# A linear-attention and long-convolution kernel on one core: other first loads, one kind of inverse tile, a new order of all steps

## The chip, the cores and the metric

The kernel runs on one core of one Trainium2 chip. A core has TensorE (PE, with its weight loads PEld), VectorE (DVE), ScalarE (ACT) and GpSimd (POOL), and SyncE (SP), which here only issues transfers. Each runs its own instructions in their order and waits on semaphores for the others. The metric is the device time of one execution in microseconds (us); lower is better.

## The reference

Eight batches, eight heads, 576 positions. First a linear attention with feature maps made of exponentials, then a gated convolution over positions, done in the frequency domain:

```python
def phi(x):                                   # x: (8, 8, 576, 64), w_phi: (64, 128)
    proj = np.einsum('bhsd,df->bhsf', x, w_phi)
    proj = proj - np.max(np.abs(proj), axis=-1, keepdims=True)
    return np.concatenate([np.exp(proj), np.exp(-proj)], axis=-1)
q_p, k_p = (phi(q), phi(k))
kv = np.einsum('bhsf,bhsd->bhfd', k_p, v)
z = np.sum(k_p, axis=2)
num = np.einsum('bhsf,bhfd->bhsd', q_p, kv)
den = np.einsum('bhsf,bhf->bhs', q_p, z)[..., None] + 1e-06
x = num / den                                 # then laid out as (8, 576, 512)
...
proj = x @ w_proj                             # (512, 1536): x1, x2, x3
X2 = np.fft.rfft(x2, n=S, axis=1)
H = np.fft.rfft(filter_fft, n=S, axis=0)[None, :, :]
x2_conv = np.fft.irfft(X2 * H, n=S, axis=1)
out = (x1 * x2_conv * x3) @ w_out             # float32
```

## The kernel before

One batch after the other passes through a chain of steps, and the chains of neighbouring batches are interleaved. Nothing plans at run time: a long text, PLAN, names every step in the order in which it is issued, with its batch and tile, the engine where there is a choice, and the PSUM bank behind an @. run() goes through the words and calls the method of that name. Each engine executes its share of the words in this order; a step waits only for the data and buffers that it needs.

The steps of a batch b (tiles v, m or c run over 0 to 3):

- load and loadh bring q, k and v with a cast to bf16, from GpSimd's queue; loadh brings half the heads. They fill kn, qn and vn, two buffers each. trh (L602) transposes half a batch into kT or qT on SP's queue; for batch 0, pt and pte do it on TensorE with an eviction.
- Pk and Qn (matmuls with w_phi), then maxk and maxq (VectorE, the absolute maxima, L707); a suffix t is the tail of the 576 positions. mhi, mlo, trm and trme turn the maxima of q into mT, which Pq subtracts inside its own matmuls. ex (ScalarE, L693) takes exponentials of both signs. em scales by the maxima of k, vs (L749) scales v by it, KV and KVe make the 128 x 65 sums.
- NE, rc and xn divide numerator by denominator. trx (L816) and trxt (L821) transpose the result x into xT and xTt by transfer; in batch 0 ptx does three of four on TensorE.
- f1 and f2 (L846, L852) fold x, F and Fe transform it to frequencies (XF), X2 multiplies by the middle third of w_proj, Y1 multiplies by the filter's spectrum, m3 (L911) sums. X1 and X3 (L919) are the outer thirds, tm multiplies them into x1s.
- The inverse transform of a tile m of 128 channels comes in two kinds. I is six matmuls into two banks for even and odd parts; Ie copies one to SBUF on ScalarE (L990), Ip and Im add and subtract the other on VectorE (L993), and ym multiplies by x1s on GpSimd or VectorE (L1038). J is ten matmuls that give the sum and the difference at once (L1028), with four more rows of the constants inv made by gen_neg and gen_ends, and yj multiplies both by x1s in one VectorE instruction (L1032). 21 tiles are of the first kind and 11 of the second.
- O multiplies by w_out (L1049), Oe evicts the product into one of four buffers o, and st (L1058) writes it out in two halves from SP's queue, each half under its own transfer.

The filter is prepared once: eight fl_load and one fl_loadt (L476, L482) read it on SP's queue, fa (L488) adds and subtracts its mirrored parts on GpSimd, rev (L499) reverses by a float32 matmul, fb, ft, Ff and Ffe transform it, and H and He give the spectrum. Constants for the transforms are made on GpSimd (gi_*), VectorE (cols_*, ang, frac) and ScalarE (sin). wz are matmuls on zeros with no use of their result.

Of the kernel before, what the change touches and what calls it, by code (L numbers as in the profile page):

```python
# [37 lines left out]
pt,k,0,0,1@3 sin,0 maxq,0,0@4 Pk,0,0@0 pte,ACT,k,0,0,1@3 pt,k,0,1,1@6 fa,POOL,1 pt,k,0,1,0@7
maxk,0,0@0 pte,ACT,k,0,1,1@6 Qn,0,2@4 pte,ACT,k,0,1,0@7 pte,DVE,q,0,1,1@2 maxq,0,2@4 Pk,0,1@6
Qn,0,3@2 ft,POOL fa,POOL,0 maxq,0,3@2 ex,k,m,0,0@0 wz,9@4 Qnt,0@4 ex,k,p,0,0@0 maxqt,0@4 Pk,0,2@2  # L40
maxk,0,2@2 ex,k,m,0,1@6 Pk,0,3@4 w_load,proj,1 rev@0 ex,k,p,0,1@6 maxk,0,3@4 mhi,0 ex,k,p,0,2@2
maxk,0,1@6 ex,k,m,0,2@2 one Pkt,0@6 mlo,DVE,0 ex,k,m,0,3@4 trm,0@2 wz,1@3 maxkt,0@6 trh,q,1,0
fb,0@0 trme,ACT,0@2 wz,12@3 em,m,0,0 ex,k,p,0,3@4 vs,POOL,m,0,0 Pq,0,1@2 trh,q,1,1 fb,1@0 em,p,0,0
exkt,m,0@6 Pq,0,2@4 exkt,p,0@6 ex,q,m,0,1@2 wz,25@0 trh,k,1,0 vs,POOL,p,0,0 ex,q,p,0,1@2 Qn,1,0@0
wz,14@6 trh,k,1,1 em,m,0,1 ex,q,p,0,2@4 maxq,1,0@0 Pq,0,3@2 w_load,proj,2 KV,0,0@6 ex,q,m,0,2@4
vs,DVE,m,0,1 em,p,0,1 ex,q,p,0,3@2 Ff,1@4 vs,POOL,p,0,1 KVe,DVE,0,0@6 Pk,1,1@0 ex,q,m,0,3@2
Ffe,DVE,1@4 Qn,1,3@6 ex,k,m,1,1@0 maxq,1,3@6 NE,0,1@4 Ff,0@2 w_load,proj,0 maxk,1,1@0 KV,0,1@6
Ffe,ACT,0@2 load,v,1 rc,0,1@4 ex,k,p,1,1@0 gen_ends,POOL Pq,0,0@2 xn,0,1@4 KVe,DVE,0,1@6 Qnt,1@4
trx,0,1 ex,q,m,0,0@2 Pk,1,0@0 maxqt,1@4 Ff,2@6 load,k,2 ex,q,p,0,0@2 maxk,1,0@0 NE,0,3@4 load,q,2
Ffe,ACT,2@6 NE,0,0@2 rc,0,3@4 ex,k,p,1,0@0 xn,0,3@4 NE,0,2@6 rc,0,0@2 Pqt,0@4 xn,0,0@2 ex,k,m,1,0@0  # L50
rc,0,2@6 ptx,0,3@2 f1,POOL,0,0,0 xn,0,2@6 exqt,p,0@4 ptx,0,0@3 Ff,3@0 exqt,m,0@4 ptxe,DVE,0,3@2
ptx,0,2@6 ptxe,DVE,0,0@3 f1,POOL,0,0,1 Ffe,ACT,3@0 Qn,1,2@4 ptxe,DVE,0,2@6 Pk,1,3@2 maxq,1,2@4
NEt,0@0 ex,k,m,1,3@2 f1,POOL,0,1,0 Pkt,1@6 exkt,m,1@6 rct,0@0 wz,27@4 maxk,1,3@2 f2,POOL,0,0,0
exkt,p,1@6 X1,0,0@5 Hl,ACT maxkt,1@6 H,0@4 f2,POOL,0,0,1 ex,k,p,1,3@2 xnt,0,0@0 H,2@6 xnt,0,1@0
He,DVE,0,0@4 f1,POOL,0,1,1 Qn,1,1@0 em,m,1,0 He,ACT,2,0@6 Pk,1,2@2 maxq,1,1@0 H,1@7 X1e,ACT,0,0@5
# [140 lines left out]
class Kernel:  # L196
# [273 lines left out]

    def fl_load(self, i, a):
        self.nc.sync.dma_start(  # L476
# [638 lines left out]
```

## Time and profile before

| what | us |
|---|---|
| median of 3 runs | 312.28 |
| lowest and highest run | 309.18, 315.27 |
| span of the profiled execution, first to last instruction | 311.6 |

The profiled execution's time is known by its span alone, which lies 0.7 below the median of the runs and within their spread. In the profile a busy engine is one with an instruction in flight; matmuls overlap, so the busy time of PE is larger than the time that each adds to a queue of them. A group's line gives busy time and the mean of one, then the idle time of its engine ahead of it and what ended most of it. Rows of a timeline give start, length, engine and line; brackets at the end give the idle time ahead and what ended it. PEclk is the share of TensorE's full clock that was granted.

### The profile page before, as it was taken

How to read it: one execution, taken by the hardware profiler on the slowest of the kernel's cores; microseconds unless marked ns; L12 is line 12 of the kernel's file. 1: busy time of each engine (PE TensorE's matmuls, PEld its weight loads, DVE VectorE, ACT ScalarE, POOL GpSimd, SP SyncE). 2: the span in 40 equal slices, each digit the busy share in tenths (PEclk: the TensorE clock that was granted, in tenths of full speed). 3: DMA queues.
4: the chain of work that ended last, by engine and by line, in shares of the span. 5: the costliest groups of instructions: out<-in, count | busy, mean ns of one | idle time of the engine just before them, and what ended most of it. 6: DMA issues, size and time to landing. Idle time of an engine off the chain costs nothing.

```text
span 311.6 us, 10240 instructions
## 1 busy us (share of the span) xinstructions
PE 281.0 (90%) x4331; PEld 205.3 (66%) x4360; DVE 268.6 (86%) x447; ACT 216.3 (69%) x345; POOL 203.8 (65%) x163
## 2 busy tenths in 40 slices
PE   1968977999999996999899799999999999999992
PEld 0534665778667874687577677587578767786761
DVE  6997999699988884978897888799999999998863
ACT  1898997797668764499679469883837898834230
POOL 8446877668673975667958667977259877674040
PEclk9978999899999998999999999999999999999998
DMA  7999999799799869696695999998350252060046
GB/s 162 235 203 159 136 202 193 105 190 133 91 164 204 94 110 170 116 160 107 114 198 82 131 160 153 172 175 160 84 117 4 56 93 69 19 110 21 1 115 192
DMA packets 72735, 40.20 MB, mean 129 GB/s; under 512 B 53040, under 2 KB 67504, under 8 KB 72688
## 3 DMA queue, kind: packets, MB, share of 16 engines
q1 hardware_dynamic: 57472, 22.62, 40.2%
q0 software_dynamic: 14816, 16.25, 34.5%
q10 hardware_dynamic: 400, 0.66, 0.8%
q8 instruction: 34, 0.56, 0.8%
q14 instruction: 13, 0.11, 0.1%
HBM read 33.75 MB, written 9.44 MB: 139 GB/s over the span
## 4 chain that ended last, share of the span: by engine, by line
PE 70%; DVE 12%; DMA 7%; ACT 5%; issue 3%; SPq 1%; POOL 0%; DVEq 0%; POOLq 0%
PE ps L919 16%; PE ps L897 10%; PE ps L1049 8%; PE ps L764 5%; PE ps L972 4%; PE ps L778 4%; DMA xT<-xn 4%; DMA out_dram<-o 3%; PE ps L1028 3%; PE ps L858 3%; PE ps L862 3%; PE ps L928 2%; DVE mq L707 2%; PE ps L665 2%; PE ps L638 2%
## 5 line engine op out<-in xcount | busy, mean ns | idle before, releaser
L919 PE MATMUL ps<-xT,wproj 128*128 128x256 bf16 x512 | 65.8, 275 | 4.3 <-DVE x1s L960 2.3
L919 PEld LDWEIGHTS <-wproj 128*128 128x128 bf16 x512 | 48.6, 98 | 14.5 <-issue 5.1
L707 DVE TENSOR_REDUCE mk<-ps 128x8 f32<-128x1024 f32 (+1 forms) x40 | 44.0, 1110 | 5.9 <-ACT HTo L295 2.2
L707 DVE TENSOR_REDUCE mq<-ps 128x8 f32<-128x1024 f32 (+1 forms) x40 | 44.0, 1110 | 5.5 <-PE ps L638 4.5
L749 POOL TENSOR_TENSOR vm<-vn,vm 128x1152 bf16<-128x1152 bf16 x14 | 30.4, 2178 | 18.2 <-ACT vm L743 18.2
L749 POOL TENSOR_TENSOR vp<-vn,vp 128x1152 bf16<-128x1152 bf16 x16 | 34.8, 2180 | 10.5 <-ACT vp L743 10.3
L911 POOL TENSOR_TENSOR T<-T,T 128x1024 bf16<-128x1024 bf16 x12 | 25.5, 2124 | 21.9 <-DVE T L907 21.8
L693 ACT ACTIVATE Ekp<-ps 128x1024 bf16<-128x1024 f32 x32 | 32.8, 1030 | 6.6 <-DVE mk L707 3.3
L1038 POOL TENSOR_TENSOR yT<-cv,x1s 128x576 bf16<-128x576 f32 x19 | 24.3, 1289 | 18.3 <-DVE x1s L964 12.8
L852 POOL TENSOR_TENSOR xf<-SD 128x512 bf16<-128x512 bf16 x27 | 31.2, 1170 | 6.7 <-DVE SD L846 5.3
L693 ACT ACTIVATE Ekm<-ps 128x1024 bf16<-128x1024 f32 x32 | 32.8, 1033 | 3.6 <-DVE mk L707 2.7
L693 ACT ACTIVATE Eqm<-ps 128x1024 bf16<-128x1024 f32 x32 | 32.9, 1034 | 3.1 <-PE ps L671 2.9
L1049 PE MATMUL ps<-wout,yT 128*128 128x512 bf16 x133 | 34.3, 385 | 0.7 <-issue 0.2
L693 ACT ACTIVATE Eqp<-ps 128x1024 bf16<-128x1024 f32 x32 | 32.5, 1031 | 3.4 <-PE ps L671 3.3
L846 POOL TENSOR_TENSOR SD<-xn 128x512 bf16<-128x512 bf16 x23 | 26.5, 1160 | 12.6 <-DVE xn L797 12.6
L897 PE MATMUL ps<-wproj,XF 128*128 128x512 bf16 x117 | 30.3, 380 | 0.7 <-issue 0.2
L295 ACT CAST x1s<-ps 128x512 bf16<-128x512 f32 (+1 forms) x30 | 16.0, 548 | 13.1 <-PE ps L928 8.4
L797 DVE TENSOR_TENSOR xn<-ps,r 128x512 bf16<-128x512 f32 x32 | 22.0, 689 | 1.1
L1049 PEld LDWEIGHTS <-yT 128*128 128x128 bf16 x144 | 13.4, 99 | 14.1 <-issue 0.6
L990 ACT COPY es<-ps 128x288 f32<-128x288 f32 x21 | 8.5, 404 | 20.3 <-PE ps L972 19.8
L960 DVE TENSOR_TENSOR x1s<-ps,x1s 128x512 bf16<-128x512 f32 x32 | 21.7, 683 | 0.6 <-ACT x1s L295 0.4
L778 PE MATMUL ps<-KVs,Eqp 128*128 128x65 bf16 x256 | 19.6, 192 | 2.2 <-DVE mq L707 0.6
...
## 6 DMA issues: line engine op xcount, KB each, us to landing
out_dram<-o SPq DMA_DIRECT2D x67, 128.0 KB, 2.9
vn<-in_v_dram POOLq DMA_DIRECT2D x8, 576.0 KB, 7.5
kn<-in_k_dram POOLq DMA_DIRECT2D x7, 576.0 KB, 9.7
qn<-in_q_dram POOLq DMA_DIRECT2D x7, 576.0 KB, 6.6
...
fl<-in_moe_filter_fft_dram SPq DMA_DIRECT2D x8, 128.0 KB, 5.8
out_dram<-o ACTq DMA_DIRECT2D x5, 128.0 KB, 2.8
...
```

The lines of the kernel that those rows point to most:

```text
L693: self.nc.scalar.activation(e, p, AF.Exp, bias=0.0, scale=1.0 if g == "p" else -1.0)
L707: self.nc.vector.tensor_reduce(out=out, in_=src, axis=AX.X, op=ALU.max, apply_absolute_value=True)
L749: self.eng(eng).tensor_tensor(out=t[:, :, :, 0:64], in0=self.at("vn", b)[:, 2 * X:2 * X + 2], in1=t[:, :, :, 64:65].to_broadcast([128, 2, ...
L778: self.mm(self.pb(u, 65 * a, 65 * a + 65), E, KVs[:, u, v, s, :], start=(s == 0), stop=(s == 1))
L797: self.nc.vector.tensor_tensor(out=o, in0=n[:, :, :, 0:64], in1=self.at("r", 4 * b + v).to_broadcast([128, 2, 4, 64]), op=ALU.mult)
L846: self.eng(eng).tensor_tensor(out=o[:, :, 2 * i:2 * i + 2, :], in0=x[:, :, 0:2, :], in1=x[:, :, 2:4, :], op=ALU.subtract if i else ALU.add)
L852: self.eng(eng).tensor_tensor(out=o[:, :, 2 * i:2 * i + 2, :], in0=x[:, :, 0:4:2, :], in1=x[:, :, 1:4:2, :], op=ALU.subtract if i else ALU ...
L897: self.mm(self.pb(0), l, w[:, kt, 512:1024], start=(kt == 0), stop=(kt == 3))
L911: self.eng(eng).tensor_tensor(out=Y, in0=Y, in1=self.at(f"T{2 * e + 1}", b), op=ALU.add)
L919: self.mm(o[:, d], w[:, kt, f0 + 128 * m:f0 + 128 * m + 128], y[:, 1, ::-1, ::-1] if d else y[:, 0], start=(kt == 0), stop=(kt == 3))
L1038: self.eng(eng).tensor_tensor(out=self.at("yT", b)[:, m, 0:SEQ], in0=self.turn_of("cv", (b, m)).rearrange("p x h t -> p (x h t)"), in1=sel ...
L1049: self.mm(self.pb(0), y[:, kt, 128 * c:128 * c + 128], w[:, kt, :], start=(kt == 0), stop=(kt == 3))
```

## The change

The change has four parts.

1. The first loads come in another order and at other times. On GpSimd's queue q of batch 0 (first half), k of batch 1, q (second half), k of batch 0 in halves, q of batch 1, v of batch 0. The filter's loads no longer stand at the front of SP's queue: a new step, hold, writes one column of fl and flt on VectorE, and as each filter load writes over it, it must wait for that.
2. Every inverse tile is of the six-matmul kind: the 11 J become I with Ie, Ip, Im and ym, and gen_neg, gen_ends, J, yj and four of the ten rows of inv go.
3. There are five buffers o in place of four.
4. PLAN is a new text: all steps stand in a new order, and for some the engine or the bank is another (VectorE has 12 of the 36 evictions Oe, 17 before; 3 of 32 f2, 5 before; 2 of 16 m3, 4 before; 7 of 32 ym, where it had 2 of 21).

```diff
-RING = {'Ekp': 4, 'Ekm': 4, 'Eqp': 3, 'Eqm': 3, 'vp': 3, 'vm': 3, 'r': 4, 'o': 4, 'kn': 2, 'qn': 2,
+RING = {'Ekp': 4, 'Ekm': 4, 'Eqp': 3, 'Eqm': 3, 'vp': 3, 'vm': 3, 'r': 4, 'o': 5, 'kn': 2, 'qn': 2,
...
-fl_load,2,1 cols_h loadh,q,0,0 zeros fl_load,3,0 gi_part loadh,q,0,1 ident fl_load,0,0 cols_i
+loadh,q,0,0 gi_part gz,DVE ident pt,q,0,0,1@2 pt,q,0,0,0@5 w_load,phi load,k,1 loadh,q,0,1 cols_i
...
-        R("inv", [128, 10, 288], BF16)
+        R("inv", [128, 6, 288], BF16)
...
+    def hold(self):
+        self.nc.vector.memset(self.fl[:, 0:4:2, 0:1], 0.0)
+        self.nc.vector.memset(self.flt[:, 0:1], 0.0)
...
-    def gen_neg(self, eng):
...
-    def gen_ends(self, eng):
...
-    def J(self, b, m):
-        c, inv = slice(128 * m, 128 * m + 128), self.at("inv")
-        for h in range(2):
-            ks = [(self.at("T0", b)[:, 0, c], 0), (self.at("T0", b)[:, 1, c], 1),
-                  (self.at("T2", b)[:, 0, c], 6 if h else 2),
-                  (self.at("T2", b)[:, 1, c], 7 if h else 3), (self.at("T4", b)[:, c], 8 + h)]
-            for i, (l, t) in enumerate(ks):
-                self.mm(self.pb(h, 0, 288), l, inv[:, t, :], start=(i == 0), stop=(i == 4))
-
-    def yj(self, b, m):
...
```

What the new order does at two places follows, as the queues of single engines; a number behind a name is that of its buffer, and the L is the line in the version that the row belongs to.

The start, SP's queue, before: the filter's loads and the small w_phi, then the transposes of batch 1.

```order
L476 DMA fl<-in_moe_filter_fft_dram 32x2x512 x5
L576 DMA phi<-in_w_phi_dram 64x128 x2
L482 DMA flt<-in_moe_filter_fft_dram 64x512
L476 DMA fl<-in_moe_filter_fft_dram 32x2x512 x3
L602 DMA_TRANSPOSE qT_82<-qn_76 128x9x128 x2
L602 DMA_TRANSPOSE kT_84<-kn_78 128x9x128 x2
L816 DMA_TRANSPOSE xT_132<-xn_129 128x4x128
```

SP's queue at the same place, after:

```order
L583 DMA phi<-in_w_phi_dram 64x128 x2
L483 DMA fl<-in_moe_filter_fft_dram 32x2x512 x3
L609 DMA_TRANSPOSE kT_84<-kn_78 128x9x128
L483 DMA fl<-in_moe_filter_fft_dram 32x2x512 x5
L609 DMA_TRANSPOSE kT_84<-kn_78 128x9x128
L489 DMA flt<-in_moe_filter_fft_dram 64x512
L609 DMA_TRANSPOSE qT_82<-qn_76 128x9x128 x2
L823 DMA_TRANSPOSE xT_132<-xn_129 128x4x128
```

The filter's loads now have the two transposes of k of batch 1 between them, and its tail flt stands behind both.

The start, VectorE, before: the maxima of q and k of batch 0 (mq, mk), evictions of transposes (qT, kT), and the cast f of the filter's tail.

```order
L297 COPY kT_83<-ps 128x640
L707 TENSOR_REDUCE mq_87<-ps 128x2x4
L707 TENSOR_REDUCE mk_85<-ps 128x2x4
L297 COPY qT_81<-ps 128x512
L707 TENSOR_REDUCE mq_87<-ps 128x2x4
L297 CAST f_150<-flt 64x512
L707 TENSOR_REDUCE mq_87<-ps 128x2x4
L707 TENSOR_REDUCE mq_87<-ps 128x2x2
L707 TENSOR_REDUCE mk_85<-ps 128x2x4 x3
```

VectorE at the same place, after:

```order
L714 TENSOR_REDUCE mk_85<-ps 128x2x4
L714 TENSOR_REDUCE mq_87<-ps 128x2x4
L309 MEMSET mh_89 128x64
L309 MEMSET mh_90 128x64
L300 COPY kT_83<-ps 128x640
L300 COPY kT_83<-ps 128x512
L714 TENSOR_REDUCE mq_87<-ps 128x2x2
L300 CAST f_150<-flt 64x512
L714 TENSOR_REDUCE mk_85<-ps 128x2x4 x3
```

The cast f moved behind the last maximum of q; three maxima of k follow it as a block.

Batches 0 to 2, SP's queue, before: the transposes of x of batch 2 (xT, xTt) and the stores of batch 0 (out_dram), two halves from each buffer o, after the first three.

```order
L602 DMA_TRANSPOSE qT_81<-qn_75 128x9x128
L1058 DMA out_dram<-o_1123 64x512
L816 DMA_TRANSPOSE xT_132<-xn_129 128x4x128 x4
L821 DMA_TRANSPOSE xTt_134<-xnt_130 128x2x128
L1058 DMA out_dram<-o_1122 64x512 x2
L1058 DMA out_dram<-o_1123 64x512
L602 DMA_TRANSPOSE kT_83<-kn_77 128x9x128
```

SP's queue at the same place, after:

```order
L823 DMA_TRANSPOSE xT_132<-xn_129 128x4x128
L1035 DMA out_dram<-o_1111 64x512
L609 DMA_TRANSPOSE qT_81<-qn_75 128x9x128
L823 DMA_TRANSPOSE xT_132<-xn_129 128x4x128 x3
L1035 DMA out_dram<-o_1114 64x512
L1035 DMA out_dram<-o_1111 64x512
L1035 DMA out_dram<-o_1112 64x512
L1035 DMA out_dram<-o_1113 64x512 x2
L1035 DMA out_dram<-o_1112 64x512
L1035 DMA out_dram<-o_1114 64x512
L609 DMA_TRANSPOSE kT_83<-kn_77 128x9x128
```

All stores of batch 0 but one now stand behind the four transposes xT of batch 2, and ahead of xTt.

The inverse tiles of batch 1, VectorE, before: half sums cv of two tiles, and two yj (yT from ps).

```order
L993 TENSOR_TENSOR cv_1118<-es_1116,ps 128x9x32
L960 TENSOR_TENSOR x1s_140<-ps,x1s_140 128x2x8x32
L993 TENSOR_TENSOR cv_1119<-es_1117,ps 128x9x32 x2
L993 TENSOR_TENSOR cv_1118<-es_1116,ps 128x9x32
L1032 TENSOR_TENSOR yT_1121<-ps,x1s_140 128x2x9x32
L707 TENSOR_REDUCE mk_86<-ps 128x2x4
L1032 TENSOR_TENSOR yT_1121<-ps,x1s_140 128x2x9x32
```

VectorE at the same place, after:

```order
L1000 TENSOR_TENSOR cv_1107<-es_1105,ps 128x9x32 x2
L1000 TENSOR_TENSOR cv_1108<-es_1106,ps 128x9x32 x2
L1015 TENSOR_TENSOR yT_1110<-cv_1107,x1s_140 128x576
L810 RECIPROCAL rt_127<-ps 128x8
L1000 TENSOR_TENSOR cv_1107<-es_1105,ps 128x9x32
L816 TENSOR_TENSOR xnt_130<-ps,rt_127 64x256 x2
L1000 TENSOR_TENSOR cv_1107<-es_1105,ps 128x9x32
L714 TENSOR_REDUCE mk_86<-ps 128x2x4
L1000 TENSOR_TENSOR cv_1108<-es_1106,ps 128x9x32 x2
```

All four tiles are made of half sums now, through two buffers cv, and one of the four products is VectorE's.

More of the change, by code (lines that the diff above doesn't have):

```diff
@@ L38 @@
[L38 to L55, printed above, removed]
@@ new lines @@
+pt,k,0,1,0@3 wz,1@4 pt,k,0,1,1@4 maxq,0,2@6 zeros pte,DVE,k,0,1,0@3 pte,DVE,k,0,1,1@4 ex,k,p,0,0@0
+fa,POOL,0 pte,ACT,k,0,0,1@5 Qnt,0@5 Pk,0,2@2 maxqt,0@5 ex,k,m,0,0@0 ex,k,p,0,2@2 ft,POOL maxk,0,2@2
+Pk,0,1@6 wz,14@0 wz,25@5 wz,26@1 Pk,0,3@4 ex,k,m,0,1@6 ex,k,p,0,1@6 ex,k,m,0,2@2 mhi,0 maxk,0,3@4
+ex,k,m,0,3@4 ex,k,p,0,3@4 maxk,0,1@6 mlo,DVE,0 fa,POOL,1 rev@0 Pkt,0@6 trm,0@3 trme,ACT,0@3 Pq,0,1@2
+maxkt,0@6 em,p,0,0 vs,DVE,p,0,0 fb,0@0 fb,1@0 em,m,0,0 exkt,p,0@6 exkt,m,0@6 wz,12@6 Pq,0,2@4
+ex,q,m,0,1@2 ex,q,p,0,1@2 em,p,0,1 Qn,1,0@6 Pq,0,3@2 ex,q,m,0,2@4 ex,q,p,0,2@4 em,m,0,1 load,v,1
@@ L193 @@
+st,ACT,7,0,1 st,SP,7,0,0
 """
```

313 lines of the change are left out of this document (156 added, 157 removed).

## Prediction

> **What bounds the kernel now.** I read first the page's busy shares, then the busy time of each engine by stretches, then the groups by shape, the timeline of the first 60 us, and last the waits of TensorE. The page:
>
> ```profile
> span 311.6 us, 10240 instructions
> ...
> PE 281.0 (90%) x4331; PEld 205.3 (66%) x4360; DVE 268.6 (86%) x447; ACT 216.3 (69%) x345; POOL 203.8 (65%) x163
> ```
>
> A share over the whole span mixes stages, so the same by stretches (columns: stretch, length, busy time of PE, PEld, DVE, ACT, POOL, granted clock, DMA):
>
> ```profile
> core 0: us, PE busy (x) PEld busy (x) DVE busy (x) ACT busy (x) POOL busy (x), PEclk, DMA share, GB/s
> 0.00:60.00 60.00, 44.13 (x682) 30.13 (x687) 51.97 (x116) 46.29 (x76) 39.71 (x45) 0.91 1.02 176
> 60.00:200.00 140.00, 132.82 (x2070) 97.59 (x2085) 119.83 (x178) 106.12 (x168) 100.15 (x75) 0.99 0.90 143
> 200.00:220.00 20.00, 18.97 (x386) 15.30 (x387) 18.38 (x31) 12.62 (x19) 14.31 (x11) 1.00 0.98 148
> 220.00:280.00 60.00, 59.06 (x999) 44.94 (x1000) 57.42 (x91) 42.98 (x68) 42.15 (x29) 1.00 0.35 68
> 280.00:300.00 20.00, 19.95 (x177) 14.61 (x176) 16.78 (x29) 6.76 (x14) 5.73 (x5) 1.00 0.18 40
> 300.00:312.00 12.00, 6.05 (x30) 2.73 (x28) 4.19 (x7) 1.48 (x3) 1.70 (x2) 0.89 0.57 154
> ```
>
> From 60 to 300 us TensorE is busy 230.8 of 240 us, so there its work is the time, with 9.2 us of gaps. From 220 to 280 VectorE is nearly as full (57.42 of 60). Before 60 us no engine is full: the first loads, VectorE and ScalarE hand work to each other.
>
> **The change: inverse tiles.** The eleven tiles that J and yj made are made by I, Ie, Ip, Im and ym. The chain of waits gives the pace of the two kinds of tile back to back (start, length, what), and the groups by shape give the rest:
>
> ```profile
> 70.33 1.23 PE ps L1028 x10
> ...
> 72.05 1.47 PE ps L972 x12
> ```
>
> ```profile
> L1038 POOL TENSOR_TENSOR yT<-cv,x1s 128x576 bf16<-128x576 f32 x19 | 24.3, 1289 | 18.3 <-DVE x1s L964 12.8 <-DVE cv L993 5.4
> ...
> L993 DVE TENSOR_TENSOR cv<-es,ps 128x288 f32<-128x288 f32 x42 | 17.3, 446 | 4.2 <-ACT es L990 3.8
> ...
> L1028 PE MATMUL ps<-inv,T 128*128 128x288 bf16 x110 | 15.3, 286 | 0.0
> ...
> L990 ACT COPY es<-ps 128x288 f32<-128x288 f32 x21 | 8.5, 404 | 20.3 <-PE ps L972 19.8 <-DVE xn L797 0.3
> ...
> L1032 DVE TENSOR_TENSOR yT<-ps,x1s 128x576 bf16<-128x576 f32 x11 | 8.3, 753 | 0.7 <-PE ps L1028 0.2
> ...
> L1038 DVE TENSOR_TENSOR yT<-cv,x1s 128x576 bf16<-128x576 f32 x2 | 1.5, 753 | 0.0
> ```
>
> A matmul of either tile costs 0.123 us (1.23/10, 1.47/12). Four fewer in each of eleven tiles: 44 x 0.123 = 5.4 us less for TensorE. Against it ScalarE gets 11 copies (11 x 0.404 = 4.4 us); VectorE loses 11 x 0.753 = 8.3, gets 22 half sums (22 x 0.446 = 9.8) and five more ym (5 x 0.753 = 3.8), and is relieved elsewhere in the new order (five fewer evictions of O, two fewer each of f2 and of the sums of T), so about even; GpSimd gets six more ym (6 x 1.289 = 7.7). ScalarE and GpSimd, 106.12 and 100.15 of 140, have room. By the plan seven of the eleven tiles lie in batches 0 to 3, before 200 us, where VectorE has 20 us free: their 3.4 us are gained whole. Three lie in batches 4 and 5, where VectorE has 4.2 us free in 80: of their 1.5 us I count half as lost, +0.7. The last (batch 7) lies in the final chain: J and yj took 1.23 + 0.75 there, I, copy, two half sums and ym take 0.74 + 0.40 + 0.89 + 0.75 = 2.8, beside matmuls of X3 and O that cover part: between 0 and +0.8, I take +0.3, since the cover is two groups of eight and four matmuls.
>
> **The fifth output buffer and the order of the stores.** TensorE's longest gap after 60 us (timelines of TensorE, VectorE and SP's queue, then the stretch after it):
>
> ```profile
> 121.20 0.28 PE L858 MATMUL ps<-Dt,xnt 128*128 128x288 bf16 x1 [2.38 <-DVE o L297]
> ```
>
> ```profile
> 120.46 0.69 DVE L297 COPY o<-ps 128x512 f32<-128x512 f32 x1 [2.99 <-DMA out_dram<-o]
> ```
>
> ```profile
> 110.75 1.25 SPq L821 DMA_TRANSPOSE xTt<-xnt  x1
> 112.05 1.87 SPq L1058 DMA_DIRECT2D out_dram<-o  x3
> ```
>
> ```profile
> 122.40:125.80 3.40, 3.40 (x28) 2.21 (x27) 1.86 (x3) 2.53 (x5) 0.00 (x0) 0.62 0.17 45
> ```
>
> The second eviction of batch 1 takes the buffer of a tile of batch 0 whose second store stands third in SP's row at 112.05, behind the 1.25 us of the xTt transpose. That eviction waits 2.99, TensorE 2.38, and then 3.40 us run at a clock of 0.62, which loses 1.3 more: 3.7 in all. With five buffers the first eviction of batch 1 needs no store, and the store that the second needs comes second behind the last xT transpose, ahead of xTt: 1.25 + 0.62 us earlier. The stores stay behind the transposes of batch 2, so some wait can stay, now on ScalarE. Between 0 and -3.7; I take two thirds, -2.4, because 1.9 of 2.99 go by the queue alone.
> The Trainium skill ("TensorE: Matmul & The Clock Gate", HAM oscillation) says that the clock falls after idle gaps of more than about 3.4 us. Here it fell after 2.38 us, so the trace does not bear that limit out; by the page this term would be two thirds of 2.38, 1.6, and the sum 0.8 higher.
>
> **The start.** Rows of the timeline of all engines, then landings (last number: us from issue to landing):
>
> ```profile
> 0.74 2.28 SPq L476 DMA_DIRECT2D fl<-in_moe_filter_fft_dram  x5
> ...
> 5.72 0.81 DVE L422 TENSOR_SCALAR turn<-nr,cols 128x288 f32<-128x288 f32 x2
> ...
> 7.81 0.61 DVE L448 TENSOR_SCALAR turn<-turn 128x864 int32<-128x864 int32 x1
> ...
> 13.62 4.65 POOL L488 TENSOR_TENSOR turn<-fl 128x1024 f32<-128x1024 f32 x2 [4.63 <-DMA fl<-in_moe_filter_fft_dram]
> ...
> 17.35 1.20 DVE L297 CAST f<-flt 64x512 bf16<-64x512 f32 x1
> ...
> 18.48 1.80 DVE L707 TENSOR_REDUCE mq<-ps 128x8 f32<-128x1024 f32 x2
> ...
> 20.38 3.49 DVE L707 TENSOR_REDUCE mk<-ps 128x8 f32<-128x1024 f32 x3
> ...
> 20.87 3.78 PE L499 MATMUL ps<-turn,bk 128*128 128x512 f32 x4
> ...
> 22.68 3.29 SPq L602 DMA_TRANSPOSE qT<-qn  x2
> ...
> 24.91 0.29 PE L735 MATMUL ps<-ident,mh 128*128 128x128 bf16 x1
> ```
>
> ```profile
> kn<-in_k_dram POOLq DMA_DIRECT2D x1, 576.0 KB, 12.6
> qn<-in_q_dram POOLq DMA_DIRECT2D x1, 576.0 KB, 15.0
> fl<-in_moe_filter_fft_dram SPq DMA_DIRECT2D x3, 128.0 KB, 6.5
> ```
>
> hold stands on VectorE where the row of 7.81 stood, without ang,2 ahead (0.81): about 7 us. So the filter's loads leave 6.3 us later than at 0.74. Before, first issue to last landing took 13.62 - 0.74 = 12.9 us. Low bound for the last fl now: eight issues of 0.46 (2.28/5), one transpose of 1.6 (3.29/2) between, then 6.5: 7 + 3.7 + 1.6 + 6.5 = 18.8. High bound: behind all of the first loads, which ended at 22.7 (7.7 + 15.0, the q of batch 1 that SP then transposes), and some 2 us for the filter's own bytes: 25. I take 21, about 7 + 12.9 plus the transpose. GpSimd's two fa then end at 21 + 4.65 = 25.7; the second half of rev (1.9) ends at 27.6 against 24.65, and Pkt, trm and Pq of batch 0 stand behind it. VectorE comes to ft at about 21 as before (20.3, and some copies more); flt, behind a second transpose, lands near 23, and ft (1.20) with three maxima behind it (3.49) ends at 27.7: trm at 28 against 24.91. Both ways +3.1 (low bound +1.0, high bound 25 + 4.65 + 1.9 - 24.65 = +6.9). Everything of batch 0 queues behind: Pq, the exponentials, KV, X1.
>
> Part comes back before 60 us (timelines of VectorE and TensorE, stretches):
>
> ```profile
> 49.18 2.38 DVE L852 TENSOR_TENSOR xf<-SD 128x512 bf16<-128x512 bf16 x1
> ```
>
> ```profile
> 53.34 1.87 PE L919 MATMUL ps<-xT,wproj 128*128 128x256 bf16 x8 [2.27 <-DVE x1s L960]
> ```
>
> ```profile
> 54.10:57.50 3.40, 3.40 (x28) 2.71 (x25) 1.69 (x3) 1.40 (x3) 2.49 (x2) 0.61 0.39 64
> ```
>
> VectorE's f2 (2.38 us) stood ahead of the tm on which TensorE waited 2.27, and 3.40 us at 0.61 lost 1.3 more: 3.6. The two f2 of that half go to GpSimd; one of the first half comes to VectorE, earlier, where it may cost its 2.38 again. Between 0 and -3.6; I take two thirds, -2.4, as ScalarE, idle there now, will be the late one after a later start. Start in sum: +0.7.
>
> Three loads are moved besides. v of batch 0 goes behind q of batch 1 and lands last, at about the 22.7 that q had; its readers, vs, stand behind rev and maxkt, after 28, which hides it; if it landed at 30, KV would be that much later. The weights of X1 (proj,0) go behind v of batch 1, the other two weight loads and k of batch 2. X1 waited before for the transpose (chain of waits):
>
> ```profile
> 36.70 8.74 DMA xT<-xn
> ```
>
> ```profile
> xT<-xn SPq DMA_TRANSPOSE x29, 2.7
> ```
>
> That took 8.74 us amid the loads of v, k and q, where the median of the 29 is 2.7. Now v leaves before it and two weights with it, so X1 waits for the transpose or for its own weights: between -6.0 (8.7 - 2.7) and +3.2 (one more load of 576 KB ahead of the weights: k and q of batch 1 landed at 19.5 and 22.7). I count nothing, since the nearest row, this one, stood in the same crowd.
>
> **Sum.** The other gaps from 60 to 300 are 9.2 - 2.4 = 6.8 us; the new order can close or double them, and I take +1.1 for the longer chain of each inverse tile. 311.6 - 5.4 + 0.7 + 0.3 - 2.4 + 0.7 + 1.1 = 306.6, with reading the rows to a tenth. The execution profiled shows only its span; the median of the runs, 312.28, lies 0.7 above it. So 307.3, rounded to 307.
>
> **Rivals.** *The start costs nothing.* For it: q of batch 0 has the DMA to itself until 7 us, and TensorE has room before 60. Then the low bound (+1.0), the whole 3.6 at 51 to 57 and the whole 3.7 at 121: 312.3 - 5.4 + 1.0 - 3.6 - 3.7 + 1.1 = 301.7, 302. *The filter comes late, and the kernel is slower.* Place: fl and flt behind the loads of q, k and v, rev and ft in front of all of batch 0. At the high bound (+6.9), with the clock fallen while TensorE waits (1.3), nothing back at 51 and half the wait at 121 left: 312.3 - 5.4 + 1.0 + 6.9 + 1.3 - 1.8 = 314. It decides against the change once the last fl lands after about 23. Against it: fl once landed 6.5 us after issue amid the same loads. The Trainium skill ("DMA: Bandwidth & Descriptors", Queues, rings and completion order) says that each DMA engine takes turns between the queues it has work for; that speaks for this case, as held-back loads then share to the end, and the trace agrees so far as k and q of batch 1 took 12.6 and 15.0 us. *Fewer matmuls bring nothing.* VectorE, 57.42 of 60 from 220, paces; half sums and GpSimd's ym come late for O; gaps double (+6.8): 312.3 - 5.4 + 6.8 - 1.2 = 312.5, and up to 320 if ScalarE's evictions wait too. Against it: VectorE's load stays even.
>
> **How the numbers follow.** Chances: the forecast 0.42 (304 to 310), the easy start 0.24 (302), the late filter 0.18 (311 to 318), nothing gained 0.16 (309 to 320). A measurement of this kernel tells 2% from no change, so faster means below 306.0 and slower above 318.5. Faster: 0.3 of the first, nearly all of the second, 0.36. Slower: 0.2 of the third and 0.5 of the fourth (the runs spread from 309.18 to 315.27), 0.13. Within 2%: 0.51. The range that leaves out 0.2 is 301 to 315; the forecast's own is 304 to 310.
>
> **What would show it.** L1028's successor gone and the inverse group at 192 matmuls of the same 286 ns; TensorE's busy time near 275.6; fa starting near 21 (right) or after 24 (late filter); VectorE waiting for flt ahead of f; no gap of over 1 us ahead of F in batch 2, and no 0.62 stretch after it; X2 of batch 0 at 59 to 61. I am wrong if TensorE's busy time falls by less than 4 us, if fa starts before 17, or if gaps from 60 to 300 exceed 13 us.

## The result, and the profile after

The changed kernel is slower: median 326.19 us of four runs (322.5 to 338.18) against 310.75 for the kernel before on the same chip, a ratio of 1.046 (95% interval 1.036 to 1.056). The forecast was 307 with a range of 301 to 315. The profiled execution took 322.5 us with a span of 320.6; the sum of the forecast was made against a span of 311.6, so between the two profiles 9.0 us have to be explained. The ratio stands for more, 14.3 us: the profiled execution of the changed kernel is the lowest of its four, while the span of the kernel before is high for it (its runs take 309.18 to 315.27, and where both are known a time lies 1.7 to 2.0 above its span). About 5 us of the measured difference are thus in no profile. Times of the changed order spread more than those of the kernel before, in nearly every variant below. Some executions of every kernel take some per cent longer than its others at a lower granted clock (here 338.18 us); ratios and their intervals leave these out, medians and ranges hold all.

The page of the changed kernel, as the first fence of the prediction for the one before:

```profile
span 320.6 us, 10208 instructions
...
PE 282.5 (88%) x4285; PEld 203.9 (64%) x4316; DVE 267.2 (83%) x455; ACT 222.1 (69%) x360; POOL 218.0 (68%) x173
```

TensorE has 46 instructions fewer in the records (4331 to 4285) and is busy 1.5 us longer. The stretches of the prediction say where (same columns; the last one is where the kernel before ended):

```profile
0.00:60.00 60.00, 38.55 (x520) 24.79 (x524) 44.12 (x107) 38.01 (x55) 29.91 (x37) 0.89 0.98 151
60.00:200.00 140.00, 133.14 (x2135) 98.60 (x2150) 124.61 (x191) 110.02 (x181) 109.46 (x84) 0.99 0.90 145
220.00:280.00 60.00, 57.48 (x918) 41.80 (x924) 55.20 (x84) 44.79 (x73) 45.41 (x31) 1.00 0.41 82
300.00:312.00 12.00, 11.64 (x81) 7.63 (x80) 8.80 (x17) 5.12 (x11) 4.72 (x4) 1.00 0.29 69
```

In the first 60 us TensorE is busy 38.55 where it was 44.13, with 520 matmuls where it had 682: the start is late. At the end it still works through 300 to 312 (11.64 busy, 6.05 before). A stretch cut by the clock on the wall mixes different work in the two kernels, so from here on the same work is compared. The start ends with the first X2 of batch 0; the timelines of TensorE, kernel before and kernel after:

```profile
59.44 1.90 PE L897 MATMUL ps<-wproj,XF 128*128 128x512 bf16 x7
```

```profile
68.15 1.02 PE L904 MATMUL ps<-wproj,XF 128*128 128x512 bf16 x3
```

Up to there TensorE has done the same 680 matmuls in both (681 and 680 in the records). The start lost 8.7 us; from there to the end it took 252.16 before (311.6 - 59.44) and 252.45 after (320.6 - 68.15). So two things are to be explained: the 8.7, and why nothing was gained behind.

The start of the changed kernel, timeline of all engines:

```profile
7.53 2.04 SPq L483 DMA_DIRECT2D fl<-in_moe_filter_fft_dram  x3
...
10.88 2.75 SPq L609 DMA_TRANSPOSE kT<-kn  x1
...
13.68 2.46 SPq L483 DMA_DIRECT2D fl<-in_moe_filter_fft_dram  x5
...
16.18 6.77 SPq L609 DMA_TRANSPOSE kT<-kn  x1
...
23.06 0.52 SPq L489 DMA_DIRECT2D flt<-in_moe_filter_fft_dram  x1
...
28.03 4.64 POOL L495 TENSOR_TENSOR turn<-fl 128x1024 f32<-128x1024 f32 x2 [19.52 <-DMA fl<-in_moe_filter_fft_dram]
...
30.33 2.62 DVE L300 CAST f<-flt 64x512 bf16<-64x512 f32 x1 [6.86 <-DMA flt<-in_moe_filter_fft_dram]
...
36.26 0.18 DVE L738 TENSOR_TENSOR mh<-mq,mh 128x36 bf16<-128x36 f32 x1
```

SP's row is to be read as a queue: the two transposes of k of batch 1 last 2.75 and 6.77 us, so five fl leave at 13.7 and flt at 23.1. fa starts at 28.03 (13.62 before), VectorE stands 6.86 us in front of f, with three maxima of batch 0 behind it, and mlo comes at 36.26 (24.08 before). The row is only a part of that: the last fl has left SP at about 16 and is there at 28. The five fl behind the transpose took 11.7 to 12.0 us from issue to landing, and flt 7; the transpose ahead of them, issued at 10.88, landed at 24.70, and the fl landed behind it in the order of the queue, from 26.0 to 27.6. The page's line on all eight (median from issue to landing last), which says 5.8 for the kernel before:

```profile
fl<-in_moe_filter_fft_dram SPq DMA_DIRECT2D x8, 128.0 KB, 11.7
```

Behind the start, one wait stands out. TensorE's timeline, the stretch behind the wait, and SP's queue ahead of it:

```profile
136.20 0.63 PE L935 MATMUL ps<-xTt,wproj 128*128 128x64 bf16 x16 [2.33 <-DMA xTt<-xnt]
```

```profile
136.50:139.90 3.40, 3.31 (x40) 2.33 (x37) 1.37 (x2) 0.58 (x3) 0.00 (x0) 0.55 0.98 235
```

```profile
117.95 4.39 SPq L1035 DMA_DIRECT2D out_dram<-o  x7
122.44 1.90 SPq L609 DMA_TRANSPOSE kT<-kn  x1
124.38 4.07 SPq L609 DMA_TRANSPOSE qT<-qn  x1
128.54 1.19 SPq L828 DMA_TRANSPOSE xTt<-xnt  x1
```

The wait for an output buffer (2.38 us at 121 before) is gone, and a wait of 2.33 for xTt of batch 2 with the same slow stretch behind it is there: in the new order that transpose stands behind seven stores and two transposes.

The same work between two marks, from the first product of KV with the features of q in batch 1 to that in batch 7, and from there to the end; kernel before, then after:

```profile
69.67:268.53 198.86, 189.71 (x3077) 141.02 (x3098) 175.34 (x262) 146.81 (x232) 142.69 (x102) 0.99 0.76 122
268.53:311.60 43.07, 37.47 (x453) 27.81 (x453) 31.70 (x59) 13.79 (x26) 14.61 (x11) 0.97 0.36 83
```

```profile
78.63:276.41 197.78, 187.60 (x3033) 137.60 (x3055) 174.47 (x272) 149.31 (x241) 149.66 (x109) 0.99 0.72 122
276.41:320.60 44.19, 37.83 (x451) 27.48 (x453) 30.05 (x55) 16.70 (x32) 19.90 (x15) 0.97 0.36 80
```

The middle gained 1.1 us and the end lost 1.1. In the middle TensorE is busy 2.1 less with 44 records fewer, and idle 1.0 more (198.86 - 189.71 = 9.15, and 197.78 - 187.60 = 10.18).

### The profile page after: what moved, and what is told of

The parts are those of the page before. It is cut to its first block, busy times and chain, and to the rows that moved or that the text cites. A ratio compares the mean times of both kernels' runs of the same rounds, so it can differ in the third digit from the quotient of the medians.

```text
span 320.6 us, 10208 instructions
## 1 busy us (share of the span) xinstructions
PE 282.5 (88%) x4285; PEld 203.9 (64%) x4316; DVE 267.2 (83%) x455; ACT 222.1 (69%) x360; POOL 218.0 (68%) x173
## 4 chain that ended last, share of the span: by engine, by line
PE 58%; DVE 21%; ACT 7%; DMA 6%; issue 5%; POOL 1%; DVEq 0%; POOLq 0%; ACTq 0%
PE ps L926 13%; PE ps L904 10%; PE ps L1026 6%; PE ps L771 5%; DVE mk L714 4%; PE ps L785 4%; DVE cv L1000 3%; PE ps L979 3%; PE ps L672 3%; DVE mq L714 2%; DMA xTt<-xnt 2%; PE ps L645 2%; DMA flt<-in_moe_filter_fft_dram 2%; PE ps L678 2%; DVE xn L804 2%
## 5 line engine op out<-in xcount | busy, mean ns | idle before, releaser
L1015 POOL TENSOR_TENSOR yT<-cv,x1s 128x576 bf16<-128x576 f32 x25 | 33.6, 1350 | 15.1 <-DVE cv L1000 10.9
L756 POOL TENSOR_TENSOR vm<-vn,vm 128x1152 bf16<-128x1152 bf16 x15 | 33.3, 2221 | 10.1 <-ACT vm L750 10.0
L853 POOL TENSOR_TENSOR SD<-xn 128x512 bf16<-128x512 bf16 x24 | 28.0, 1174 | 15.6 <-DVE xn L804 15.5
L756 POOL TENSOR_TENSOR vp<-vn,vp 128x1152 bf16<-128x1152 bf16 x14 | 30.2, 2154 | 8.4 <-ACT vp L750 8.3
L859 POOL TENSOR_TENSOR xf<-SD 128x512 bf16<-128x512 bf16 x29 | 32.8, 1153 | 4.4 <-DVE SD L853 3.2
L918 POOL TENSOR_TENSOR T<-T,T 128x1024 bf16<-128x1024 bf16 x14 | 29.7, 2124 | 7.2 <-DVE T L914 7.2
L1000 DVE TENSOR_TENSOR cv<-es,ps 128x288 f32<-128x288 f32 x64 | 25.9, 448 | 3.4 <-POOL yT L1015 1.9
L298 ACT CAST x1s<-ps 128x512 bf16<-128x512 f32 (+1 forms) x33 | 17.8, 550 | 14.9 <-PE ps L935 6.5
L979 PE MATMUL ps<-inv,T 128*128 128x288 bf16 x192 | 27.5, 286 | 0.4 <-DVE x1s L967 0.3
L298 ACT COPY o<-ps 128x512 f32<-128x512 f32 x24 | 13.9, 589 | 14.6 <-PE ps L1026 14.5
## 6 DMA issues: line engine op xcount, KB each, us to landing
fl<-in_moe_filter_fft_dram SPq DMA_DIRECT2D x8, 128.0 KB, 11.7
```

The lines of the kernel that those rows point to most:

```text
L298: self.nc.scalar.copy(dst, src)
L756: self.eng(eng).tensor_tensor(out=t[:, :, :, 0:64], in0=self.at("vn", b)[:, 2 * X:2 * X + 2], in1=t[:, :, :, 64:65].to_broadcast([128, 2, ...
L859: self.eng(eng).tensor_tensor(out=o[:, :, 2 * i:2 * i + 2, :], in0=x[:, :, 0:4:2, :], in1=x[:, :, 1:4:2, :], op=ALU.subtract if i else ALU ...
L918: self.eng(eng).tensor_tensor(out=Y, in0=Y, in1=self.at(f"T{2 * e + 1}", b), op=ALU.add)
L979: self.mm(self.pb(e, 0, 288), l, inv[:, 2 * e + i if i < 2 else 4 + e, :], start=(i == 0), stop=(i == 2))
L1000: self.nc.vector.tensor_tensor(out=self.turn_of("cv", (b, m))[:, :, odd, :], in0=self.turn_of("es", (b, m)).rearrange("p (x t) -> p x t", ...
```

## The experiments on the start

**e1_no_hold** takes the two writes of hold away.

```diff
-load,q,1 cols_f hold ang,2 frac,2 w_phi
+load,q,1 cols_f ang,2 frac,2 w_phi
```

> The changed kernel without the two writes of hold: the filter's loads leave as soon as SP's queue comes to them, but in the same row, three of fl, the first transpose of k of batch 1, five of fl, the second transpose, flt. Theory (the filter comes late because its loads stand behind the transposes in SP's row, which themselves wait for k of batch 1 until 10.9 us): only three of fl leave earlier, the last fl still lands near 28, fa starts near 28, X2 of batch 0 near 68, and the time stays at 322 to 326. Rival one (the writes of hold are the cost): fa starts near 20 and X2 at 60, 314 to 317. Rival two (the start is caught up later, and the loss lies in the new order behind 60 us): fa may move, the time does not.

Median 325.43, ratio 1.030 (1.022 to 1.038), span 320.6, as the changed kernel. Three fl left at 1.99, the other five at 12.26, behind the first transpose, which landed at 22.2 and the five at 22.9 to 25.3; fa started at 25.72, X2 of batch 0 at 66.07. The theory was off by 2 us on fa and X2 and right on the time: hold alone is not the cost.

**e2_transposes_behind** moves the two transposes behind the filter's loads, with hold.

```diff
-fl_load,3,1 fl_load,1,0 fl_load,2,0 trh,k,1,1 fl_load,3,0 fl_load,2,1
-fl_load,0,1 fl_load,1,1 fl_load,0,0 trh,k,1,0 fl_loadt
+fl_load,3,1 fl_load,1,0 fl_load,2,0 fl_load,3,0 fl_load,2,1 fl_load,0,1
+fl_load,1,1 fl_load,0,0 fl_loadt trh,k,1,1 trh,k,1,0
```

> The changed kernel with both transposes of k of batch 1 moved behind all nine loads of the filter; hold stays. The loads leave from 7.5 to about 12 us. Theory (transposes in SP's row): the last fl lands near 20, flt near 21, fa starts near 20, X2 of batch 0 near 61, and the time falls by about 7, to 315 to 318. Rival one (hold, that is, leaving at 7.5 into the crowd of k, q and v, is the cost): fa stays near 26 to 28, the time at 321 to 326. Rival two (the loss lies behind 60 us): fa near 20, the time unchanged.

Its timeline, and TensorE's at X2:

```profile
7.53 4.34 SPq L483 DMA_DIRECT2D fl<-in_moe_filter_fft_dram  x8
...
13.95 0.47 SPq L489 DMA_DIRECT2D flt<-in_moe_filter_fft_dram  x1
...
14.55 9.30 SPq L609 DMA_TRANSPOSE kT<-kn  x2
...
20.82 4.88 POOL L495 TENSOR_TENSOR turn<-fl 128x1024 f32<-128x1024 f32 x2 [12.32 <-ACT Ekp L700]
...
23.08 0.41 DVE L300 CAST f<-flt 64x512 bf16<-64x512 f32 x1
...
27.66 0.19 DVE L738 TENSOR_TENSOR mh<-mq,mh 128x36 bf16<-128x36 f32 x1
```

```profile
60.59 1.02 PE L904 MATMUL ps<-wproj,XF 128*128 128x512 bf16 x3
```

Median 318.38, ratio 1.016 (1.006 to 1.025), span 315.5. VectorE no longer waits for flt, and the start is 7.6 shorter (60.59 against 68.15); between these two executions 5.1 of it reach the end. Among the same loads of GpSimd's queue, but ahead of the transposes, the eight fl land sooner:

```profile
fl<-in_moe_filter_fft_dram SPq DMA_DIRECT2D x8, 128.0 KB, 6.9
```

The theory holds: the place of the transposes in SP's queue, through the row and through the landing of what stands behind them, is most of the loss of the start. It comes again in the later runs with this row of SP: X2 stands at 60.81 (e2_again), 59.87 (a1), 59.42 (c3), and 63.11 in c2. In time it is less sharp: e2's runs on this chip take 316.93 to 319.35, the two lowest of e1 322.41 and 322.71.

**e3_both** does both at once.

> The changed kernel without hold and with the transposes behind the filter's loads: all nine leave at about 2 to 7 us, ahead of most of k and q. Theory (the late filter, by either road, is the whole loss): the last fl lands by 14 to 16, fa starts near 15, X2 of batch 0 near 59 to 60, the time is that of the changed kernel less 8.7, 313 to 317, still not below the kernel before, since from X2 on both took the same 252 us. Rival (the loss lies behind 60 us, the start is caught up): 321 to 326.

Median 328.54 (321.66 to 329.75), profiled span 319.9. fa did start at 15.27, but mlo stood at 32.24 and X2 at 66.38. The theory fell: an early filter is not enough.

**e4_k1_later** puts k of batch 1 back behind k of batch 0.

```diff
-w_phi load,k,1 loadh,q,0,1 cols_i
+w_phi loadh,q,0,1 cols_i
...
-loadh,k,0,1 gi_fr load,q,1 cols_f
+loadh,k,0,1 gi_fr load,k,1 load,q,1 cols_f
```

> e3_both (no hold, transposes behind the filter's loads) with the load of k of batch 1 moved in GpSimd's queue from second place to behind the second half of k of batch 0, where the kernel before had it. In e3 the filter was on time (fa at 15.3) and yet VectorE's last step of the first maxima (mlo) stood at 32.2 and X2 of batch 0 at 66.4. Theory (the loads of the first 20 us share one rate, and what leaves ahead of q and k of batch 0, filter or k of batch 1, makes batch 0 late): mlo at 24 to 26, X2 at 59 to 61, time 312 to 316. Rival (the place of k of batch 1 does not matter, the transposes of batch 1 in SP's row hold q and k up): mlo stays near 32, X2 near 66, 319 to 322.

Median 324.83, ratio 1.032 (1.019 to 1.044), span 318.2; mlo at 31.35, X2 at 63.99. The order of the loads was worth 2.4 of the 5.8 by which X2 in e3 lay behind e2, so the rival was nearer. The timeline shows what made the maxima late:

```profile
14.08 4.65 POOL L495 TENSOR_TENSOR turn<-fl 128x1024 f32<-128x1024 f32 x2 [5.52 <-DMA flt<-in_moe_filter_fft_dram]
```

```profile
15.02 1.44 DVE L354 TENSOR_TENSOR onex<-ident 128x36 bf16<-128x36 bf16 x1
16.50 2.26 DVE L355 SCALAR_TENSOR_TENSOR one<-onex 128x18 bf16<-128x18 bf16 x1
```

Two tiny steps of VectorE that take 0.17 and 0.18 us in e2 took 1.44 and 2.26 while GpSimd ran fa.

**e6_one_later** moves them out of its way.

```diff
-load,v,0 pte,DVE,q,0,1,1@5 one pte,DVE,q,0,1,0@7
+load,v,0 pte,DVE,q,0,1,1@5 pte,DVE,q,0,1,0@7
...
-maxk,0,1@6 mlo,DVE,0
+maxk,0,1@6 one mlo,DVE,0
```

> e4_k1_later with VectorE's two small steps of one moved from the middle of the first maxima to just ahead of mlo. In e4 they took 1.44 and 2.26 us beside GpSimd's two fa, against 0.17 and 0.18 in e2, where GpSimd stood idle. Theory (they were stretched by fa, and all maxima behind them were late by 3.4): the next maxima start at 15.7 instead of 19.1, mlo at 27.5 to 28.5 instead of 31.35, X2 of batch 0 at 60 to 61.5, time 314 to 318. Rival (VectorE waits for q and k anyway, or fa stretches what now stands there): mlo above 30.5, X2 above 63, 319 to 322.

The step worked and the time did not: mlo at 27.81 as the theory had it, but X2 at 77.02 and a median of 336.98, ratio 1.084 (1.062 to 1.106). Timeline of the next 20 us:

```profile
27.52 11.45 SPq L609 DMA_TRANSPOSE qT<-qn  x2
...
45.12 0.61 PE L645 MATMUL ps<-wphi,qT 64*128 64x128 bf16 x8 [13.93 <-DMA qT<-qn]
```

The two transposes of q of batch 1 last 11.45 us together on SP's row (8.77 in e4, 5.18 in e2), and TensorE stands 13.93 us for them, in front of work of batch 0. The theory was right about VectorE and blind to the next late transfer. With batch 0 earlier, GpSimd's further loads leave earlier too: the second weights at 32.3 and k of batch 2 at 37.4, against 36.2 and 41.2 in e4. That these loads slow the transposes is argued from the order of the rows; no run took them away.

**e5_readers_late** leaves the loads of the changed kernel and moves the filter's readers.

```diff
-Pk,0,2@2 maxqt,0@5 ex,k,m,0,0@0 ex,k,p,0,2@2 ft,POOL maxk,0,2@2
+Pk,0,2@2 maxqt,0@5 ex,k,m,0,0@0 ex,k,p,0,2@2 maxk,0,2@2
...
-maxk,0,1@6 mlo,DVE,0 fa,POOL,1 rev@0 Pkt,0@6 trm,0@3
+maxk,0,1@6 mlo,DVE,0 Pkt,0@6 trm,0@3
...
+vs,POOL,m,0,0 fa,POOL,0 fa,POOL,1 load,v,1
...
+KVe,DVE,0,0@0 ft,POOL rev@0 fb,0@0 fb,1@0 Ff,1@4
```

> The changed kernel with its loads, hold and SP's row as they are, but with the filter's readers later: ft, rev and fb behind KV of the first half of batch 0 (just ahead of Ff, which needs them), and the two fa behind the first vs on GpSimd, with the load of v of batch 1 and the first weight load kept behind fa. The filter lands as late as before (fl near 28, flt near 30). Theory (the delay is made by engines that run in order and wait for the filter ahead of work of batch 0): mlo at 26 to 28 instead of 36.3, the first trm near 28 instead of 36.7, KV near 36, X2 of batch 0 at 60 to 63, time 314 to 318. Rival (q, k and v of batch 0 are late themselves, so waiting for the filter cost little): mlo above 33, X2 above 65, 320 to 326.

```profile
27.91 0.18 DVE L738 TENSOR_TENSOR mh<-mq,mh 128x36 bf16<-128x36 f32 x1
...
35.73 0.70 DVE L300 CAST KVs<-ps 128x520 bf16<-128x520 f32 x1 [1.54 <-PE ps L771]
```

mlo comes 8.35 earlier and the eviction of KV 8.45 (44.18 in the changed kernel), with the filter as late as there: the waiting of in-order engines made the delay of batch 0. The times were 319.84 to 340.93, and the profiled execution is the one of 340.93, where X2 stood at 70.11; so how much of the gain reaches X2 is not shown; the lowest time is 2.7 below the changed kernel's lowest.

## The experiments behind the start

**b1_inverse_only and b2_inverse_only**: the kernel before with the eleven tiles of ten matmuls turned into tiles of six. In b1 the half sums of three tiles took a buffer still in use, so those tiles' values change; b2 mends it.

```diff
-J,5,0@0
+I,5,0@0 Ie,5,0@0
...
-yj,5,0@0
+Ip,5,0@0 Im,5,0@0 ym,DVE,5,0
```

> The kernel before, in its own order, with the eleven tiles of J and yj made by I, Ie, Ip, Im and ym at the same places (six of the new ym on GpSimd, five on VectorE), and nothing else changed. If the 44 matmuls fewer are time (the forecast's term): 5.4 less and 0.3 to 1.0 back, 306 to 307.5. Rival (they bring nothing, because the copy, the half sums and ym come late for O, or because TensorE waits for something else there): TensorE's busy time falls by 5 to 6 and its idle time rises as much, 310 to 313.

> b1_inverse_only again, with the copies and half sums of three tiles (1,2; 3,0; 4,3) moved so that no buffer of a half sum is taken before its reader: the computation is whole again. Theory from b1 (the tiles of six matmuls are not cheaper where they stand: copy, half sums and ym come late for O and for the banks, and TensorE waits): 318 to 324, from KV of batch 1 to KV of batch 7 some 205 us where the kernel before took 198.9. Rival (b1's loss came from the mixed buffers): 306 to 312.

b1: ratio 1.033 (1.025 to 1.040). b2: median 326.69, ratio 1.050 (1.041 to 1.058). The middle of b2, and VectorE's largest wait there (us in total, times, longest):

```profile
70.38:283.44 213.06, 192.53 (x3038) 140.05 (x3059) 181.00 (x276) 150.39 (x242) 151.04 (x108) 0.96 0.69 114
```

```profile
DVE cv L997 <- POOL yT L1042: 8.0, 7, 2.3
```

40 matmuls fewer (39 in the records), and 14.2 us longer than the 198.86 before: TensorE is idle 20.5 instead of 9.15, and its clock is 0.96, so its remaining work lasts longer too. Of that idle time it stands 5.1 us for half sums and 2.7 for the products of ym, waits that the kernel before does not have.

**b4_ym_vector** moves six of the eleven new products from GpSimd to VectorE.

```diff
-ym,POOL,4,0
+ym,DVE,4,0
```

> b2_inverse_only with the six ym that stood on GpSimd (of the eleven new tiles) on VectorE: 6 x 0.753 = 4.5 us more there, 6 x 1.29 = 7.7 less on GpSimd. Theory (GpSimd's products hold the buffers of the half sums, VectorE waits 8.0 us for them, O and the banks wait behind): VectorE's wait for GpSimd's ym falls below 3, from KV of batch 1 to KV of batch 7 202 to 207 us instead of 213, the time 315 to 320. Rival (it is the longer chain of copy, half sums and product itself, whoever runs it): the stretch stays above 209, the time at 322 to 327.

Median 324.86, ratio 1.045 (1.034 to 1.056), the middle 212.03 us, VectorE's wait for products still 5.0. The theory fell: it is not GpSimd's share of the products. That it is the longer chain in that order is what is left; no run took the chain alone away.

**a1_J_back and c2_J_back**: the ten-matmul tiles put back into the new order, on e2 and on c1. In a1 the tile (7,2) is multiplied by x1s before its last tm; c2 has that step behind the last tm and also gives O of tile (6,1) another bank.

```diff
-I,5,0@0 Ie,5,0@0
+J,5,0@0
...
-Im,5,0@0 Ip,5,0@0 ym,DVE,5,0
+yj,5,0@0
```

> e2_transposes_behind with the eleven tiles of ten matmuls back: J where I stood, yj in place of the second half sum, no copy and no ym for them, ten rows of constants. Five output buffers and all the rest of the order stay. If 44 matmuls at 0.123 us are time: 5.4 slower than e2, 322 to 325 (spans 320 to 321). If the six-matmul tiles bring nothing, because TensorE only waits more: as e2, 316.5 to 319.5. If they cost more than they save: 312 to 316.

> c1_xTt_ahead with the eleven ten-matmul tiles back (J where I stood, yj in place of the half sums, in the last batch behind tm), five output buffers as there. If 44 matmuls at 0.123 us are time once no other wait hides them: 4 to 5.5 above c1. If they are worth a third (from a1, whose stretch from KV of batch 1 to KV of batch 7 took 198.2 without the wait for xTt, against 196.5 hoped for c1): 1 to 2.5 above c1. If they bring nothing: within 1 of c1.

a1: 1.025 (1.010 to 1.039) beside e2's 1.016 (1.006 to 1.025), with the lower span of the two, 312.9 against 315.5. c2: 1.028 (1.012 to 1.044) beside c1's 1.027 (1.012 to 1.041). The middle of e2, then of a1:

```profile
71.07:271.42 200.35, 188.26 (x3032) 137.47 (x3055) 174.44 (x272) 149.50 (x241) 149.79 (x109) 0.99 0.74 121
```

```profile
70.35:268.57 198.22, 190.35 (x3073) 140.60 (x3095) 175.64 (x261) 145.72 (x231) 137.32 (x100) 1.00 0.75 122
```

41 matmuls more keep TensorE busy 2.1 us longer, and it is idle 7.9 instead of 12.1 us. By the ratios a1 would be 3.0 us above e2 and c2 0.3 above c1, each with an interval of some 1.5% on either side, about as wide as the 5.4 in question; by the profiled spans a1 is 2.6 below e2. So the tiles of six save 3 us here at the most that any pair says, and nothing by the others. Part of a1's 2.1 us in the middle is not the tiles: between the KV products of batches 2 and 3 e2 takes 37.09 us, with 2.23 of waiting for xTt, and a1 35.32 without that wait; over the rest of the middle the two take 163.26 and 162.90. So outside that stretch these two executions show no gain from the tiles of six. What they save in time, these runs do not settle.

**c1_xTt_ahead, e2_again and c3_xTt_look**: e2 with xTt of batch 2 ahead of the stores, e2 again beside it, and c1 again for a trace.

```diff
-trx,2,3 st,SP,0,3,1
+trx,2,3 trxt,2 st,SP,0,3,1
```

> e2_transposes_behind with one transpose moved in SP's row: xTt of batch 2 stands right behind the last xT of that batch, ahead of seven stores of batch 0 and two transposes of k and q (in the changed kernel it issued at 128.5 behind them, TensorE waited 2.33 us for it at 136.2, and 3.9 us at a clock of 0.5 followed). Theory (this wait ate what the fifth output buffer and the six-matmul tiles saved): the wait and the slow stretch go, from KV of batch 1 to KV of batch 7 some 196.5 us instead of 200.35, the time about 4 below e2. Rival (something else is late there next: the stores, k or q of batch 4, an output buffer): the stretch shrinks by less than 1.5.

> e2_transposes_behind unchanged, beside c1 and c2 on the same chip: 4 to 7 above the kernel before, X2 of batch 0 at 60 to 61, the wait for xTt of batch 2 there again (2 to 2.5 us). If the wait came by chance, it is missing in this profile and c1 gains nothing on it.

> c1_xTt_ahead again for its trace, since the one of c1 was of a disturbed execution. Theory: no wait for xTt of batch 2 and no slow stretch behind it, from KV of batch 1 to KV of batch 7 196 to 197 us. Rival (c1 was no faster than e2 in its undisturbed times, 316.8 and 317.4 against 317.1): another wait stands in its place, and the stretch takes 199 to 201.

c1: 1.027 (1.012 to 1.041); e2 again: 1.031 (1.017 to 1.045); c3: one run of 316.88. No gain that could be measured. The wait itself comes each time: with tiles of six and xTt behind the stores it is in every trace (2.3 in the changed kernel, 3.1, 2.2, 2.7, 2.3, 4.5 and 2.2 in e1 to e6, 1.8 in e2_again). In c3 the wait for xTt is gone, and TensorE's timeline shows the next one, where the middle takes 201.11:

```profile
131.47 0.61 PE L645 MATMUL ps<-wphi,qT 64*128 64x128 bf16 x8 [3.89 <-DMA qT<-qn]
```

The rival was right: a transpose of q took the place of the transpose of x, as one late transfer in SP's row replaced another.

**b3_five_o** is the kernel before with five output buffers.

```diff
-'r': 4, 'o': 4,
+'r': 4, 'o': 5,
```

> The kernel before with five output buffers instead of four and nothing else. The forecast's term: 2.4 less (between 0 and 3.7), since the first eviction of batch 1 needs no store; the gap of 2.38 us ahead of F in batch 2 and the stretch at 0.62 behind it go or shrink. Rival (the store that the next eviction needs is as late, or another transfer takes its place): the same time as before within 1 us, with a gap of over 1 us still in front of F of batch 2 or at the next xT.

```profile
70.53:264.76 194.23, 188.08 (x3077) 140.15 (x3098) 175.48 (x262) 146.37 (x232) 142.62 (x102) 1.00 0.79 125
```

The middle takes 194.23 us, 4.6 less than before; 4.0 of it lie between the KV products of batches 2 and 3 (33.23 against 37.25), where the wait and the slow stretch stood. Neither is there. The median is 308.16 of twelve runs against 312.01 of seventeen, but the ratio is 0.998 (0.993 to 1.004). It is the lowest median of all kernels here; that it is faster than the kernel before is not shown.

## Why the prediction was wrong

**The step that failed first: "I take 21, about 7 + 12.9 plus the transpose".** The last fl let fa start at 28.03, above the high bound of 25. The working counted a transpose at 1.6 us of SP's row; they lasted 2.75 and 6.77, and flt left at 23.06, the time at which I had it landed. It also took 6.5 us for the landing of the last fl, as if nothing stood ahead of it in the queue; it took 11.9 behind the transpose. Against the low bound of 18.8 that is 3.9 us of SP's row and 5.4 of landing. The chain behind was right (VectorE waiting for flt, then three maxima of 3.47 in place of 3.49, then trm) and only started late: flt landed at 30.3 where the sum had 23, its cast took 2.62 beside fa where it had 1.20, and so trm came at 36.72 against 24.91, 11.8 where the sum had 3.1. "Part comes back" was right in kind and size: of 11.8, 3.1 are back at X2, where the sum had 2.4 of at most 3.6; between trm and X2 TensorE no longer waits 2.27 for x1s as before, and no wait there is above 0.7. So the start cost 8.7 where the sum said 0.7. The rival "The filter comes late" named the place and the point ("once the last fl lands after about 23") and had 0.18. Its start, 6.9 and 1.3, is 8.2 and close to the 8.7 measured; its 314 was too low because it kept the 5.4 us of the tiles and half a wait behind the start (-6.2 in all, where +0.3 was measured). Three slips in the working change nothing of this: by its own rows the low bound is +0.7 and not +1.0, the sum of the first rival leaves out the 0.7 and 0.3 of the tiles (302.7 with them), and the chances given for "slower" add up to 0.12, not 0.13.

**The second: "44 x 0.123 = 5.4 us less for TensorE" as time.** The group came out as written, 44 matmuls fewer at the same 286 ns. The groups of the changed kernel, inverse matmuls and the products on GpSimd:

```profile
L979 PE MATMUL ps<-inv,T 128*128 128x288 bf16 x192 | 27.5, 286 | 0.4 <-DVE x1s L967 0.3
...
L1015 POOL TENSOR_TENSOR yT<-cv,x1s 128x576 bf16<-128x576 f32 x25 | 33.6, 1350 | 15.1 <-DVE cv L1000 10.9 <-DVE x1s L967 2.2 <-DVE x1s L971 1.8
```

But from X2 on TensorE's busy time fell by 1.5 us (237.36 to 235.86) and its idle time rose by 1.8 (14.8 to 16.6). "Their 3.4 us are gained whole" assumed that room on the other engines is enough; what counts is whether the copy, the half sums and ym are done when O and the banks need them. b2 shows the price where they are not (14.2 us in the middle), a1 and c2 that the new order brings it to nothing or to a small gain. The third rival, at 0.16, is nearest to this; VectorE's load did stay even (268.6 to 267.2), so load was no evidence against it. In the changed kernel the place of the loss is known in part. From the KV product of batch 1 to that of batch 2 it takes 28.29 us (28.85 before), from there to that of batch 3 it takes 37.19 (37.25 before, 33.23 in b3 with the fifth buffer alone), and from there to batch 7 132.30 (132.76 before, 132.15 in b3). So the wait for xTt takes back what the fifth buffer gave, and elsewhere in the middle the tiles of six gain some 0.4 to 1.0 us. The rest of their 5.4 is lost without one wait that stands out, and why stays open; taking the wait for xTt away brought another.

**"The fifth output buffer", -2.4 (0 to -3.7).** Right, and under-sized at its place: b3 shows 4.0 there. In the changed kernel it was lost again to xTt, moved behind the stores: 2.33 of waiting and 3.4 us at 0.55. The forecast looked at the stores and not at which transposes the new order put behind them.

**"+0.3, the last tile" and "+1.1, other gaps".** The end took 1.1 longer (43.07 to 44.19), not 0.3; a1 with ten matmuls there took 44.33, and b2, the old order with six, 42.96; so it is the order of the end and not the kind of tile. From X2 on the terms -5.4, 0.7, 0.3, -2.4 and 1.1 make -5.7; measured is +0.3.

**The marks.** The inverse group has 192 matmuls of 286 ns as written; TensorE's busy time of 275.6 was wrong (282.5: it rose by 3.0 up to X2, where the clock stood at 0.58 and 0.52 from 30 to 36 and 36 to 45 us, and fell by 1.5 behind it); fa after 24 and VectorE waiting for flt said "late filter"; no gap of over 1 us stands ahead of F in batch 2, as written; X2 at 59 to 61 was wrong, and TensorE's busy time, which was to fall by at least 4 us, rose by 1.5; the prediction had named this as what would make it wrong.
